# GpSimd's next planned operation waits for each VectorE addition of two SBUF tensors: a linear-attention plus gated-MLP kernel on one core

## The chip, the core and the metric

One core of a Trainium2 chip runs the whole kernel in one launch. The metric is the device time of one execution in microseconds (us); the time given for a kernel is the median of several executions. The core has five engines with their own instruction queues, each worked off in order: PE (TensorE), ACT (ScalarE), DVE (VectorE), POOL (GpSimd) and SP (SyncE, which here only issues DMAs). They meet through semaphores.

## What is computed

The reference, cut to what matters; S = 2048 tokens, D = 512, H = 32 heads of 16, F = 1792, bfloat16.

```python
xn = layernorm(x)
# A: linear attention with softmax features
q, k, v = split_heads(xn @ wqkv)
phi_q = concat(softmax(q @ w_phi), softmax(-(q @ w_phi)))     # per head, 32 features
phi_k = concat(softmax(k @ w_phi), softmax(-(k @ w_phi)))
kv, z = phi_k^T @ v, sum over tokens of phi_k
a = ((phi_q @ kv) / (phi_q . z + 1e-6)) @ wo
# B: bilinear gated MLP
h = (xn @ w_gate) * (xn @ w_up)
b = h @ w_down
return x + a + b
```

## The kernel before

**Stages.** Tokens are cut into 16 tiles of 128. The kernel warms TensorE up, normalises x tile by tile (LN), and transposes it so that the model dimension lies on the partitions. While the tiles arrive it runs, per token tile t, the features of k (step names `k`, then `ke` two exponentials on ACT, `kr` the sums of the features on DVE (L923), `kc` a reciprocal on ACT, `kq` and `kp` two products on POOL (L930, L935)) and the scaled v (`vs`, DVE, L962), and adds each tile to the state on PE (`kv`). The same for q is `q`, `qe`, `qr`, `qc`, `qq`, `qp`, then a DMA transpose `qT` and the numerators `n` on PE. In between PE does the products for g and u of the MLP, and from about 116 us on the last products, h times w_down and attention times wo, for pairs of token tiles p.

**Seven products instead of eight.** The large matrix products are done in blocks of two by two with seven block products. That needs sums and differences of blocks of both factors beforehand, in SBUF. On these turns the change:

- `Xs` (function XSUMS): eight differences of halves of the transposed xn, [128 x 512] each, on DVE, at 39.6 to 46.1 us. PE's block products `b7g.0` and `b6g.0` read them.
- `Xz` (XPAIR): four more of the same size for the last quarter of the tokens, on DVE, at 97.9 to 100.4 us.
- `S3`, `S1`, `S2`, `S4` (SSUMS) with the pair's number p: sums of halves of h. POOL makes them for p below 6, DVE for p = 6 and 7 ([128 x 896] each), at 180.1 to 195.3 us.
- `w` (WSUMS, L1066), `Ts`, `To`, `So`: sums of weights and of the attention's output, on POOL.

All but `w` are recorded by the helper `sums`, so they share line 989, on DVE and on POOL alike. Of a block product on PE, `b7g.0` say, b7 is the number of the product, g or u the matrix and 0 the block of F; its results are taken from PSUM by ACT (`sd`, `s2`, `s7`, `ge`) and by DVE (`a4`, `a5` at L1086, `h` at L1080).

**What sets the order.** The program is recorded as steps with their reads and writes. A planner (`_plan`) goes through them in one global order, which is written out as a list of step numbers (`ORDER`); from it follows the order of every engine's queue. The dependencies are turned into semaphore waits afterwards. A DVE sum made by `sums` is marked `lock`: in the planner's estimate POOL does not start beside it. That alone makes no wait on the chip. A real wait is added only where the step also has `sync`: the planner then remembers the sum and makes a later POOL step depend on it. The number `slip` says how many POOL steps later that is: 1 is the next POOL step in the global order, 2 the one after it. With `slip` above 1 the next POOL step also gets a dependency on the POOL step just before it, so that POOL has to finish one before it starts the other.

```python
            for q in port:
                if q[2] and last_pool is not None and last_pool not in st.deps:
                    st.deps.append(last_pool)
                q[2] = False
                q[1] -= 1
                if q[1] <= 0 and q[0] not in st.deps:
                    st.deps.append(q[0])
            port = [q for q in port if q[1] > 0]
```

In the kernel before, `sync` holds for sums given an explicit priority, which among the twenty sums on DVE are the eight S sums of pairs 6 and 7, with a slip of 2. The twelve `Xs` and `Xz` have none.

Of the kernel before, what the change touches and what calls it, by code (L numbers as in the profile page):

```python
# [478 lines left out]
AB = {7: (2, 3)}  # L479
CO = {}  # L480
CH = ''
SLIP = 2
SYN = (".0", ".1")
NX = 7
ZORD = '1726453'
# [166 lines left out]
def _program(sc, layout, arena, psum, spill, A_x, A_wqkv, A_w_phi, A_wo, B_w_gate, B_w_up, B_w_down, out):  # L652
# [33 lines left out]
    def dve(fn, reads, writes, cost=None, prio=0, name="", win=60.0):  # L686
        n = max(ap.free_size() for ap in list(writes) + list(reads))
        if cost is None:
            cost = 60.0 + 1.045 * n
        return sc.step(DVE, fn, reads=reads, writes=writes, cost=cost, prio=prio, name=name, win=win)  # L690

    def pool(fn, reads, writes, cost, prio=0, name=""):
        return sc.step(POOL, fn, reads=reads, writes=writes, cost=cost, prio=prio, name=name)
# [291 lines left out]
    def parts(v):  # L985
        return [v[:, k, :] for k in range(v.shape[1])]

    def sums(eng, out_, a_, b_, op, name, prio=None):
        fn = lambda e: e.tensor_tensor(out=out_, in0=a_, in1=b_, op=op)  # L989
        n = out_.free_size()  # L990
        if eng == POOL:
            pool(fn, parts(a_) + parts(b_), parts(out_), 100.0 + 2.0 * n, name=name, prio=prio or 0)
        else:
            st = dve(fn, parts(a_) + parts(b_), parts(out_), cost=60.0 + 0.53 * n, name=name, prio=PX if prio is None else prio)
            st.lock = True
            st.sync = prio is not None
            st.slip = SLIP
            st.reserve = RX if prio is None else 0.0

# [45 lines left out]
    def XSUMS(eng):  # L1045
        X1, X2, X3, X4 = (Tx_v[:, w] for w in range(4))
        for n, (o_, a_, b_) in enumerate(((X1, xB(0, 2), xB(0, 1)), (X3, xB(1, 2), xB(0, 2)), (X2, xB(1, 2), X1),
                                          (X4, xB(1, 1), X2))):
            for k in range(2):
                sums(eng, o_[:, k:k + 1], a_[:, k:k + 1], b_[:, k:k + 1], ALU.subtract, f"Xs{n}.{k}")  # L1050
# [114 lines left out]
    def XPAIR(eng, T_v, s0, name):  # L1165
        X1, X2, X3, X4 = (T_v[:, w] for w in range(4))

        def B(k, c):
            return xnT_v[:, 2 * k:2 * k + 2, s0 + c * 256:s0 + c * 256 + 256]
        for n, (o_, a_, b_) in enumerate(((X1, B(0, 1), B(0, 0)), (X3, B(1, 1), B(0, 1)), (X2, B(1, 1), X1),  # L1170
                                          (X4, B(1, 0), X2))):
            sums(eng, o_, a_, b_, ALU.subtract, f"{name}{n}", None if eng == DVE else 0)
# [172 lines left out]
    def TSUMS():  # L1345
        for n, (o_, a_, b_) in enumerate(((T1, B12, B11), (T2, B22, T1), (T4, B21, T2), (T3, B22, B12))):
            for lo, hi in ((0, 2), (2, 4), (4, 6), (6, HF)):
                sums(POOL, o_[:, lo:hi], a_[:, lo:hi], b_[:, lo:hi], ALU.subtract, f"Ts{n}.{lo}")
# [421 lines left out]
```

## Time and profile before

| what | value |
|---|---|
| three runs | 208.77, 208.51, 208.11 us; median 208.51 |
| the profiled execution | 208.06 us in all, its span 206.3 us |
| granted TensorE clock | 1.00 |
| PE busy | 200.9 us (97%) |
| DVE busy | 175.8 us (85%) |
| POOL busy | 163.6 us (79%) |
| ACT busy | 127.5 us (62%) |
| DVE sums at L989 | 20, 12.7 us busy, mean 671 ns |
| POOL sums at L989 | 92, 85.1 us busy, mean 952 ns |

The span is the time from the first to the last instruction of one profiled execution; the execution's own time is 1.76 us longer. The profile's busy time of PE is not PE at its peak, since matmuls overlap in their pipeline and their ends are modelled. Where the text below gives the times of a single step, they are those of its record in the trace, matched to the step by its place in its engine's queue.

### The profile page before, as it was taken

Reading aid. Unit: us, or ns where it says so; the run is one execution under the profiler, and the core shown is the slowest. Engines: PE = TensorE matmul, PEld = TensorE weight load, DVE = VectorE, ACT = ScalarE, POOL = GpSimd, SP = SyncE. Lnnn points to the kernel's source line nnn. Section 1 sums busy time; section 2 is a strip of 40 time slices with the busy share of each in tenths; the row PEclk is TensorE's granted clock in tenths of the full one; section 3 lists DMA queues with packets and bytes.
Section 4 is the critical chain, followed back from the end, with each engine's and each line's share of the span. In section 5 each row is a group of like instructions: output and inputs, shape, how many; then the busy total and the mean of one; then the engine's idle time right before and its main releaser. Section 6 shows DMA issues by size and latency. Waiting matters only on the chain.

```text
span 206.3 us, 4296 instructions
## 1 busy us (share of the span) xinstructions
PE 200.9 (97%) x1569; PEld 133.2 (65%) x1586; DVE 175.8 (85%) x336; ACT 127.5 (62%) x318; POOL 163.6 (79%) x215
## 2 busy tenths in 40 slices
PE   8999999999999999999999999999999999999995
PEld 2775544444455444544345678979988988998884
DVE  4745999999897899799999899699888769999952
ACT  4666899988787889788786663665653365610000
POOL 4065677449999989999989999999999989996100
PEclk9999999999999999999999999999999999999999
DMA  5999944899002200225672332984965749454212
GB/s 142 332 242 373 337 97 97 192 335 253 7 0 102 102 3 2 102 51 95 182 234 53 105 78 49 144 215 122 253 164 136 149 146 161 134 127 85 71 38 89
DMA packets 52277, 28.87 MB, mean 140 GB/s; under 512 B 37664, under 2 KB 50464, under 8 KB 52256
## 3 DMA queue, kind: packets, MB, share of 16 engines
q1 hardware_dynamic: 51584, 28.27, 53.1%
q10 hardware_dynamic: 672, 0.33, 0.5%
q8 instruction: 12, 0.20, 0.4%
q14 instruction: 9, 0.07, 0.1%
HBM read 13.91 MB, written 5.77 MB: 95 GB/s over the span
## 4 chain that ended last, share of the span: by engine, by line
PE 91%; DVE 5%; ACT 1%; issue 1%; DVEq 0%
PE ps L711 88%; DVE arena L989 2%; PE ps L1536 2%; ACT arena L672 1%; DVE arena L923 1%; DVE arena L1395 1%; DVE arena L1210 0%; DVE arena L1080 0%; DVE arena L1329 0%; DVE arena L962 0%; DVEq L455 0%; DVE arena L1458 0%; DVEq L426 0%; DVE arena L1021 0%
## 5 line engine op out<-in xcount | busy, mean ns | idle before, releaser
L711 PE MATMUL ps<-arena 128*128 128x256 f16 (+5 forms) x1559 | 196.7, 287 | 2.1 <-DVE arena L989 0.4
L711 PEld LDWEIGHTS ps<-arena 128*128 128x128 f16 (+1 forms) x1576 | 131.9, 98 | 67.4 <-DVE arena L1080 2.0
L672 ACT ACTIVATE arena<-ps 128x512 bf16<-128x512 f32 (+3 forms) x184 | 91.6, 538 | 45.2 <-PE ps L711 30.5
L989 POOL TENSOR_TENSOR arena<-arena 128x512 f16<-128x512 f16 (+4 forms) x92 | 85.1, 952 | 8.0 <-DVE arena L834 3.8
L923 DVE TENSOR_REDUCE arena<-arena 128x64 f32<-128x1024 bf16 x32 | 38.7, 1210 | 2.2 <-ACT arena L672 2.2
L935 POOL TENSOR_TENSOR arena<-arena 128x512 bf16<-128x512 bf16 x32 | 34.0, 1067 | 0.4
L1066 POOL TENSOR_TENSOR arena<-arena 128x512 f16<-128x512 bf16 (+1 forms) x28 | 32.3, 1161 | 2.3 <-ACT arena L672 1.1
L672 ACT ACTIVATE arena<-arena 128x32 f32<-128x32 f32 (+4 forms) x96 | 28.4, 314 | 5.4 <-DVE arena L923 3.8
L1395 DVE TENSOR_TENSOR arena<-ps,arena 128x256 bf16<-128x256 f32 (+1 forms) x56 | 22.8, 418 | 6.3 <-PE ps L711 5.6
L1080 DVE TENSOR_TENSOR arena<-ps,arena 128x512 f16<-128x512 f32 x28 | 19.2, 686 | 0.7 <-PE ps L711 0.2
L672 ACT ACTIVATE ps<-ps 128x512 f32<-128x512 f32 x21 | 12.2, 585 | 4.2 <-PE ps L711 2.1
L832 DVE BATCH_NORM_STATS2 arena<-arena 128x6 f32<-128x512 bf16 x16 | 10.5, 674 | 4.3 <-DMA arena<-in_A_x_dram 4.2
L1210 DVE TENSOR_TENSOR arena<-ps,arena 128x256 f16<-128x256 f32 x28 | 11.3, 416 | 3.4 <-ACT arena L672 3.2
L930 POOL TENSOR_TENSOR arena<-arena 128x32 f32<-128x32 f32 x32 | 8.5, 268 | 6.6 <-ACT arena L672 6.6
L989 DVE TENSOR_TENSOR arena<-arena 128x512 f16<-128x512 bf16 (+1 forms) x20 | 12.7, 671 | 0.1
L1086 DVE TENSOR_TENSOR arena<-ps,arena 128x512 bf16<-128x512 f32 x14 | 9.6, 687 | 2.9 <-ACT arena L672 1.5
L962 DVE TENSOR_TENSOR arena<-ps,arena 128x512 bf16<-128x512 f32 x16 | 10.9, 682 | 0.2 <-PE ps L711 0.2
L1329 DVE TENSOR_TENSOR arena<-ps,arena 128x512 bf16<-128x512 f32 x16 | 10.9, 680 | 0.1
L1214 DVE TENSOR_TENSOR ps<-ps,arena 128x512 f32<-128x512 f32 x14 | 9.6, 690 | 0.8 <-PE ps L711 0.5
L1086 DVE TENSOR_TENSOR ps<-ps,arena 128x512 f32<-128x512 f32 x14 | 9.7, 692 | 0.6 <-ACT arena L672 0.6
L814 POOL TENSOR_TENSOR arena<-arena 128x128 bf16<-128x128 bf16 x4 | 1.6, 426 | 8.5 <-DMA arena<-in_A_w_phi_dram 8.5
L1021 DVE TENSOR_TENSOR arena<-ps,arena 128x512 f16<-128x512 f32 x10 | 6.7, 684 | 0.4 <-PE ps L711 0.3
(25 smaller groups left out, 36.5 us busy)
## 6 DMA issues: line engine op xcount, KB each, us to landing
spill<-arena SPq DMA_DIRECT2D x7, 512.0 KB, 2.7
arena<-spill SPq DMA_DIRECT2D x7, 512.0 KB, 3.9
arena<-in_A_x_dram SPq DMA_DIRECT2D x6, 512.0 KB, 5.5
arena<-in_B_w_down_dram SPq DMA_DIRECT2D x2, 896.0 KB, 6.6
out_dram<-arena SPq DMA_DIRECT2D x14, 128.0 KB, 1.9
arena<-in_B_w_gate_dram SPq DMA_DIRECT2D x1, 768.0 KB, 7.6
arena<-in_B_w_up_dram SPq DMA_DIRECT2D x1, 768.0 KB, 7.7
arena<-arena SPq DMA_TRANSPOSE x44, 3.1
```

What stands on the lines that cost most here:

```text
L672: return e.activation(out=out_ap, in_=in_ap, func=func, scale=scale, **kw)
L711: ins = e.matmul(o, lhsT=l, rhs=r, start=s, stop=p, skip_group_check=True)
L923: dve(lambda e: e.tensor_reduce(out=sm, in_=Et.rearrange("p (c h f) -> p c h f", c=8, f=16), axis=AX.X, op=ALU.add), [Et], [sm], cost=1130 ...
L935: pool(lambda e: e.tensor_tensor(out=ev[:, :, 1, :], in0=ev[:, :, 1, :], in1=ratio[:, :, None].to_broadcast([128, H, 16]), op=ALU.mult), [ ...
L962: dve(lambda e: e.tensor_tensor(out=o1, in0=src, in1=rp_[:, :, :, None].to_broadcast([128, 8, 4, 16]), op=ALU.mult), [src, rs_v[:, t % 4, ...
L989: fn = lambda e: e.tensor_tensor(out=out_, in0=a_, in1=b_, op=op)
L1066: pool(lambda e, o_=o_, a_=a_, b_=b_, op=op: e.tensor_tensor(out=o_, in0=a_, in1=b_, op=op), [a_, b_], [o_], 100.0 + 2.09 * 512, name=f"w{ ...
L1080: dve(lambda e: e.tensor_tensor(out=h, in0=src, in1=g, op=ALU.mult), [src, g], [h], name=f"h{ft}.{sg}", prio=PD)
L1086: dve(lambda e: e.tensor_tensor(out=o, in0=src, in1=sn, op=ALU.add), [src, sn], [o], name=name, prio=PD)
L1210: dve(lambda e: e.tensor_tensor(out=h, in0=src, in1=g, op=ALU.mult), [src, g], [h], cost=328.0, name=f"zh{f}.{c}", prio=PB)
L1329: dve(lambda e: e.tensor_tensor(out=ov, in0=src, in1=wv4[:, :, :, None].to_broadcast([128, 8, 4, 16]), op=ALU.mult), [src, w], [o], cost=6 ...
L1395: dve(lambda e: e.tensor_tensor(out=out_, in0=in_ps, in1=in_sb, op=ALU.add), [in_ps, in_sb], [out_], cost=328.0, name=f"{name}.{p}")
```

## The change

All twenty DVE sums now carry `sync`, and the slip is 1: the POOL step that comes next after a sum in the global order waits for that sum. The dependency of a POOL step on the POOL step before it, which went with a slip of 2, is no longer added. The global order, the engines' queues and every computation stay as they are.

```diff
-SLIP = 2
+SLIP = 1
...
             st = dve(fn, parts(a_) + parts(b_), parts(out_), cost=60.0 + 0.53 * n, name=name, prio=PX if prio is None else prio)
             st.lock = True
-            st.sync = prio is not None
+            st.sync = True
             st.slip = SLIP
             st.reserve = RX if prio is None else 0.0
```

In the planned order the POOL steps that follow the sums are these:

| DVE sums | next POOL step (waits after) | wait of before |
|---|---|---|
| Xs1.0, Xs0.0, Xs0.1, Xs1.1 | kq3 | none |
| Xs2.1, Xs2.0, Xs3.0 | kq4 | none |
| Xs3.1 | w3.2 | none |
| Xz0 | qq2 | none |
| Xz2, Xz1, Xz3 | qp2 | none |
| S3.6 | So1.5 | So3.5 |
| S1.6, S3.7, S2.6 | S4.5.3 (fourth sum of pair 5, second part) | So1.6 |
| S4.6, S1.7 | So2.6 | So4.6 |
| S2.7 | So4.6 | none left |
| S4.7 | none left | none left |

## The prediction

> **What bounds the kernel.** I read the page first, then the chain of waits, then both engines of the change in the timeline.
>
> ```profile
> span 206.3 us, 4296 instructions
> PE 200.9 (97%) x1569; PEld 133.2 (65%) x1586; DVE 175.8 (85%) x336; ACT 127.5 (62%) x318; POOL 163.6 (79%) x215
> ```
>
> PE is the bound. So the change can gain only where PE stands still, and can lose wherever it makes PE stand still. The chain that ended last shows where another engine holds PE; its columns are start, us, what:
>
> ```profile
> 39.65 2.38 DVE arena L989 x4
> 42.02 0.04 issue
> 42.07 1.72 PE ps L711 x14
> ...
> 98.33 2.03 DVE arena L989 x3
> 100.36 0.61 DVE arena L1080
> 100.97 0.05 issue
> 101.02 1.47 PE ps L711 x6
> ```
>
> Both places are runs of DVE sums at L989: first Xs, which PE's b7g.0 waits for, then Xz, behind which DVE's h5.1 (L1080) is queued, which PE's k14 waits for. To size PE's standstill I take the starts of successive matmuls less 213 ns, which is the spacing of the 512-column ones elsewhere. It is 0.57 us before b7g.0 at 42.07, 0.17 before k5 at 43.80, 0.50 before k14 at 101.02 and 0.26 before k15 at 102.35. Other pieces over 0.15 us after 10 us are nearly all of 0.22, a missing record each.
>
> Why the sums are late shows in the timeline (start, us, engine), DVE then POOL, and in the group of Xs:
>
> ```profile
> 39.65 2.37 DVE L989 TENSOR_TENSOR arena<-arena 128x512 f16<-128x512 bf16 x4
> ```
> ```profile
> 39.60 0.27 POOL L930 TENSOR_TENSOR arena<-arena 128x32 f32<-128x32 f32 x1 [1.48 <-ACT arena L672]
> 39.95 1.12 POOL L935 TENSOR_TENSOR arena<-arena 128x512 bf16<-128x512 bf16 x1
> ```
> ```profile
> L989 DVE TENSOR_TENSOR arena<-arena x8: 409/456/1272, 39.6 to 45.5; 128x512 f16<-128x512 bf16 x8
> ```
>
> The same sum takes 409 to 1272 ns. The long one is Xs0.0, 40.07 to 41.34: it lies beside kp3 (39.95 to 41.07) and ends 0.28 us behind it. Xz1 does the same beside qp2 (98.68 to 99.96, qp2 ends 99.68: again 0.28), and S3.7 beside S4.5.3 (1570 ns, against 611 for S4.6 with nothing beside it). It goes the other way too: S4.5.3 begins while S1.6 runs and takes 1413 ns against 1150, and So1.5 behind S3.6 929 against 667. So whichever of the two began first keeps the other waiting nearly to its end. Three sums lose 0.86, 0.86 and 0.96 us in this way.
>
> **The change part by part.** The wait makes the order of the plan real: kq3 waits for four Xs, kq4 for three, qq2 and qp2 for the Xz, four POOL steps near the end for S sums.
>
> First place, Xs. With kq3 held, the four sums run at their undisturbed pitch (0.335 us, as Xs0.1 to Xs1.1) from 39.65, so Xs1.1 ends at 39.65 + 3 x 0.335 + 0.41 = 41.06 instead of 42.01. b7g.0 is then ready before PE is: 0.57 gone. DVE goes on 0.95 earlier with kr4 and vs3 (to 42.85 instead of 43.74), so k5's 0.17 is gone as well, minus about 0.03 of normal spacing: 0.7 us. What is late next: kq3, from 39.60 to 41.06 + 0.14 = 41.20 (0.14 us lies between the end of S1.7 and So4.6, which waits for it); kp3 then ends at 42.6, not 41.07, and nb14 and nb15, queued behind it, at 43.2, not 42.14. Their readers come later: kv3 at 50.07, nm14 at 46.32, nm15 at 48.73. kq4 was idle for 2.26 us before 44.40, waiting for ACT's kc4; all that is early brings kc4 to about 43.8 and Xs3.0 to 43.96, so kq4 starts near 44.1. Xs3.1 then meets kp4 and is held to 45.75, before b4g.0 needs it (46.8). w3.2 begins 0.25 us behind b7u.0 on PE, hence 0.7 earlier too; S1.0.3 behind it can't start before the transpose xT13 lands at 47.12 (before: 47.76, directly behind w3.2), so POOL enters the next stretch 0.6 earlier. Thus all engines move together:
>
> ```profile
> 47.00:97.00 50.00, 49.68 (x293) 24.20 (x298) 44.74 (x62) 40.66 (x97) 49.03 (x55) 1.00 0.26 66
> ```
>
> (Columns: stretch, length, busy PE, PEld, DVE, ACT, POOL, granted clock, DMA.) PE and POOL are both full here, and PE's smallest reserves against POOL are 0.14 (w3.4 to b7g.4 at 79.9) and 0.25 us (kp5 to kv5 at 61.4). POOL being 0.1 behind PE's move fits in. I keep 0.69 at 97.
>
> Second place, Xz. Undisturbed they end at 99.42 instead of 100.36; h5.1 ends at 100.02, h12.1 at 101.35, so the 0.50 and 0.26 go. From there DVE's own queue (qr3, kr14, h5.2) is 0.73 earlier, and PE's b1u.6 waits for it with 0.05 to spare: gain 0.73. The price is on POOL:
>
> ```profile
> 98.49 1.18 POOL L935 TENSOR_TENSOR arena<-arena 128x512 bf16<-128x512 bf16 x1
> 99.64 0.45 POOL L930 TENSOR_TENSOR arena<-arena 128x32 f32<-128x32 f32 x1
> 100.04 1.33 POOL L1066 TENSOR_TENSOR arena<-arena 128x512 f16<-128x512 bf16 x1
> 101.33 1.05 POOL L935 TENSOR_TENSOR arena<-arena 128x512 bf16<-128x512 bf16 x1
> ```
>
> qp2 starts at 99.56, 1.07 later; qp2, kq13 and w4.6 get back 0.12, 0.18 and 0.17 of their own stretching, so what is queued behind them (kp13, kp12, S2.0.3 ...) is about 0.6 late (1.07 - 0.12 - 0.18 - 0.17). kv12 on PE has 1.37 us against kp12, which the delay and PE's gain just use up. The transpose qT2 on SP, with a spill store and a load behind it, waits for qp2; the nearest reader of the load has 3.5 us. At 106.99 POOL idles 0.73 us before qq3, and 0.15 before kq15 at 110.61; that takes up the delay and leaves POOL 0.28 ahead of its old place, PE wanting 0.73 (the first part moves both alike). kv14 has 0.30 against kp14, of which 0.05 is signalling: 0.73 - 0.28 - 0.25 = 0.2 comes back there as a new stall, and 0.53 is left of this place.
>
> Third place, the end. S3.7 and S2.6 are 0.95 earlier, S4.5.3 ends at 188.5 instead of 187.2; P3.5 needs it at 192.2. So2.6 is held until S1.7, that is from 189.8 to about 191.6; P6o.6 needs it at 194.8. So4.6 behind it is 0.9 late; P3o.6 comes at 200.5. PE waits there only for c22.5 before P3.5, about 0.1: gain 0.1. The dropped waits of POOL on itself (0.12 us of idle time each, three of them) are hidden under POOL's slack at the end. Each added wait instruction costs POOL at least nothing and at most the 0.08 idle seen before a held step; that is in the 0.14.
>
> Sum: 0.69 + 0.53 + 0.1 = 1.32. Against its own execution 208.06 becomes 206.7; that execution is 0.45 below the median, and from the median 208.51 I get 207.2.
>
> The Trainium skill, SBUF — State Buffer, "Who interferes with whom", calls the shared pair of ports an exclusive lock, held for a whole instruction by the one that issued first, and lets DVE operations with two SBUF inputs take part. The rows above agree. By this rule the wait saves no time on the ports, it only moves it from DVE to POOL; with POOL as the bound it would give the last rival's time.
>
> **The rivals.** One: the first gain is lost again in the stretch from 47 to 97. The waits put w3.2's idle 0.78 us to a transpose (L1066 waiting for arena<-arena), and xT12 does land at 46.61. If that, and not b7u.0, starts POOL, POOL is not earlier, and b7g.4 cuts PE's gain to 0.1. Then the sum is 0.1 + 0.5 + 0.1 = 0.7: 207.8. Against it: w3.2 reads nothing of xT12; S1.0.3 behind it does.
>
> Two: nothing measurable. PE regains the stalls and gives them up at other waits with 0.05 us to spare, of which there are some thirty; 208.5.
>
> Three, slower: POOL's delay reaches PE through kp. If the Xz do not shorten (their length then has another cause than their neighbour), qp2 starts at 100.36 + 0.14, 2.0 late; kp12 ends 1.66 late, and kv12 with its 1.37 stalls 0.35; past the 0.73 and 0.15 of idle time 0.78 is left, kv14 with 0.25 stalls 0.53 in all. No gain at the first place either: 208.51 + 0.5 = 209.0. It decides once POOL is over 1.37 us late against PE at kv12 or 0.30 at kv14. For it: POOL is 98% busy from 47 to 97. Against it: twice 0.28 us between the neighbour's end and the sum's.
>
> **How the numbers follow.** Forecast 0.50, rival one 0.18, rival two 0.15, rival three 0.17. A difference of about 0.3% (0.6 us) is what can be told from none. Rival one lies just beyond that bound; forecast and rival one make faster 0.68, rival two same 0.15, rival three slower 0.17. Low end: all of PE's stalls go, 0.70 + 0.76 + 0.15 = 1.6, so 206.9, less 0.3 for the spread of the runs (208.11 to 208.77): 206.6. High end: rivals one and two are in, 208.7; left out is most of rival three. The forecast's own range is 206.8 to 207.5.
>
> **What would show it.** Right: no DVE sum of 512 columns over 0.6 us except Xs3.1; Xs1.1 ends near 41.1; b7g.0, k5, k14 and k15 without standstill; qp2 about 1 us behind qc2's end; PE's piece at 47 to 97 moved by 0.7. Wrong: PE waiting for L935 (kp) at kv12 or kv14; kp5 or w3.4 as PE's releaser; sums as long as before.

## The result and the profile after

The changed kernel takes 206.64 us (median of six runs), the kernel before 208.65 in the same comparison: ratio 0.990, interval 0.988 to 0.992, so 2.0 us faster (1.6 to 2.5). The prediction was 207.2 us, with a range of 206.8 to 207.5 for the forecast alone and 206.6 to 208.7 with its rivals, and a gain of 1.3 us. Two more comparisons, told below as experiments, gave 0.994 (0.992 to 0.996) and 0.992 (0.989 to 0.995). A ratio here is worked out from all runs of its comparison; it is not the quotient of the two medians and differs from it by up to 0.0013. Over all four sets of runs the median of 24 runs with the change is 206.62 and of 92 without it 208.06: 1.45 us.

The page, first lines:

```profile
span 205.1 us, 4301 instructions
PE 200.1 (98%) x1569; PEld 133.2 (65%) x1586; DVE 173.6 (85%) x336; ACT 127.3 (62%) x318; POOL 162.6 (79%) x215
```

DVE is 2.2 us less busy with the same 336 instructions. The chain that ended last (start, us, what) no longer leaves PE at either place:

```profile
30.17 10.74 PE ps L711 x49
40.91 0.05 issue
40.96 7.19 PE ps L711 x53
...
92.14 9.27 PE ps L711 x49
101.41 0.05 issue
101.46 8.22 PE ps L711 x51
```

The two breaks of 0.05 us that it still lists there are matmuls whose record is missing (in v3 and in k15), not waits. The group of the eight Xs, and the timeline of DVE and of POOL at the first place:

```profile
L989 DVE TENSOR_TENSOR arena<-arena x8: 415/418/1251, 39.8 to 44.7; 128x512 f16<-128x512 bf16 x8
```
```profile
39.83 1.42 DVE L989 TENSOR_TENSOR arena<-arena 128x512 f16<-128x512 bf16 x4
...
42.93 1.21 DVE L989 TENSOR_TENSOR arena<-arena 128x512 f16<-128x512 bf16 x3
...
44.66 1.25 DVE L989 TENSOR_TENSOR arena<-arena 128x512 f16<-128x512 bf16 x1
```
```profile
41.33 0.27 POOL L930 TENSOR_TENSOR arena<-arena 128x32 f32<-128x32 f32 x1 [3.04 <-ACT arena L672]
41.68 1.06 POOL L935 TENSOR_TENSOR arena<-arena 128x512 bf16<-128x512 bf16 x1
...
44.23 0.27 POOL L930 TENSOR_TENSOR arena<-arena 128x32 f32<-128x32 f32 x1 [0.50 <-DVE arena L989]
```

The first four sums take 1.42 us instead of 2.37, and kq3 (L930) starts behind them, at 41.33 instead of 39.60. The profile puts its wait down to ACT, but ACT's kc3 had ended at 39.70; Xs1.1 ended at 41.25, 0.08 us before kq3 starts, and that is the wait that was added. The one long sum left, 1251 ns, is Xs3.1 beside kp4.

The four Xz at the second place, first in the kernel before, then with the change:

```profile
97.88 2.48 DVE L989 TENSOR_TENSOR arena<-arena 128x512 f16<-128x512 bf16 x4
```
```profile
97.31 1.60 DVE L989 TENSOR_TENSOR arena<-arena 128x512 f16<-128x512 bf16 x4
```

POOL there, with the change:

```profile
98.99 1.05 POOL L935 TENSOR_TENSOR arena<-arena 128x512 bf16<-128x512 bf16 x1 [0.69 <-DVE arena L989]
100.01 0.26 POOL L930 TENSOR_TENSOR arena<-arena 128x32 f32<-128x32 f32 x1
100.23 1.15 POOL L1066 TENSOR_TENSOR arena<-arena 128x512 f16<-128x512 bf16 x1
101.34 1.06 POOL L935 TENSOR_TENSOR arena<-arena 128x512 bf16<-128x512 bf16 x1
```

qp2 is held until the Xz are done; behind it kq13 and w4.6 are back at 0.26 and 1.15 us (0.45 and 1.33 before), so that kp13 starts at 101.34, as before (101.33). PE, though, comes to kv12, which needs the next product kp12, 1.16 us earlier than in the trace before (103.62 instead of 104.77).

To compare two traces I take the start of one PE step in both. The steps just ahead of the first place differ already: v3, which reads no sum and starts before the first of them ends, lies between 39.73 and 40.51 us in twelve profiled executions of all the kernels here, in no relation to the change. Behind v3 there is hardly any spread: the time of the whole execution less the start of v3 is 168.14 and 168.15 us in the two profiled executions of the kernel before, and 166.70, 166.70 and 166.68 in the three with the change. Counted from v3, the change moves PE in three stretches only:

| PE's place against the kernel before, us | first place (v3 to b5g.0) | second (q3 to b5g.6) | end (P4.5 to P4.7) | v3 to P4.7 |
|---|---|---|---|---|
| before, a second profile | 0.00 | 0.00 | -0.03 | -0.03 |
| with the change, three profiles | -0.75, -0.76, -0.75 | -0.59, all three | -0.12, -0.12, -0.11 | -1.46, all three |
| Xs alone | -0.75 | 0.00 | -0.03 | -0.78 |
| Xz alone | 0.00 | -0.59 | -0.03 | -0.62 |
| S alone | 0.00 | 0.00 | -0.11 | -0.12 |
| the sums wait instead | +0.18 | +1.12 | +0.06 | +1.45 |
| slip of 2 for all | -0.75 | -0.07 | -0.03 | -0.85 |
| qp2 later still | -0.75 | +0.28 | -0.11 | -0.47 |

The last column can differ from the sum of the others by what is lost between the second place and the end: 0.09 where the sums wait, 0.11 with qp2 later still.

### The profile page after: what moved, and what is told of

Same layout as the page of the kernel before. It is cut to its first block, busy times and chain, and to the rows that moved or that the text cites. A ratio compares the mean times of both kernels' runs of the same rounds, so it can differ in the third digit from the quotient of the medians.

```text
span 205.1 us, 4301 instructions
## 1 busy us (share of the span) xinstructions
PE 200.1 (98%) x1569; PEld 133.2 (65%) x1586; DVE 173.6 (85%) x336; ACT 127.3 (62%) x318; POOL 162.6 (79%) x215
## 4 chain that ended last, share of the span: by engine, by line
PE 92%; DMA 2%; DVE 2%; ACT 1%; issue 1%; POOL 0%; DVEq 0%; POOLq 0%
PE ps L711 92%; DMA arena<-in_B_w_up_dram 2%; ACT arena L672 1%; DVE arena L923 1%; DVE arena L1395 1%; DVE arena L1210 0%; DVE arena L1329 0%; POOL arena L778 0%; POOL arena L805 0%; DVEq L455 0%; DVE arena L1458 0%; POOL arena L777 0%; POOLq L778 0%; POOL arena L806 0%; POOLq L1755 0%
## 5 line engine op out<-in xcount | busy, mean ns | idle before, releaser
L989 POOL TENSOR_TENSOR arena<-arena 128x512 f16<-128x512 f16 (+4 forms) x92 | 84.5, 943 | 9.8 <-DVE arena L989 4.3
L935 POOL TENSOR_TENSOR arena<-arena 128x512 bf16<-128x512 bf16 x32 | 33.7, 1059 | 1.0 <-DVE arena L989 0.7
L832 DVE BATCH_NORM_STATS2 arena<-arena 128x6 f32<-128x512 bf16 x16 | 10.5, 674 | 5.2 <-DMA arena<-in_A_x_dram 5.2
L930 POOL TENSOR_TENSOR arena<-arena 128x32 f32<-128x32 f32 x32 | 8.5, 269 | 5.3 <-ACT arena L672 4.7
L989 DVE TENSOR_TENSOR arena<-arena 128x512 f16<-128x512 bf16 (+1 forms) x20 | 10.5, 562 | 0.1
```

The lines of the kernel that those rows point to most:

```text
L935: pool(lambda e: e.tensor_tensor(out=ev[:, :, 1, :], in0=ev[:, :, 1, :], in1=ratio[:, :, None].to_broadcast([128, H, 16]), op=ALU.mult), [ ...
```

## The experiments

Theory: a sum and a POOL step that overlap block each other, and the wait lets the sum go first at places where PE is behind the sum and nothing close is behind the POOL step. Against it: that POOL's delay comes back at PE; that avoiding the overlap counts, whoever waits; that the gain lies somewhere no trace shows.

**The kernel before once more.** No edit but `SLIP = 1 + 1`.

> The kernel before, unchanged: a second profile and more runs of it, since the two profiled executions differ by 1.3 us and the medians by 2.0. If the collisions of sums and GpSimd steps are the same in every execution, this profile shows Xs0.0 and Xz1 at 1.27 us again, the same standstills of PE (0.57 before b7g.0, 0.50 before k14), a span near 206.3 us and a time near 208.1. If they vary from run to run and the profiled execution was a lucky one, more sums are long here and the span is near 206.9. If the start varies (arrival of the inputs), the sums are as in the first profile and the span differs before 39 us.

208.16 us against 207.99, ratio 1.000 (0.9985 to 1.0015). The group of Xs:

```profile
L989 DVE TENSOR_TENSOR arena<-arena x8: 410/456/1275, 40.0 to 45.9; 128x512 f16<-128x512 bf16 x8
```

The same eight durations within 4 ns, and Xz1 at 1281. So the collisions of Xs and Xz belong to the order, not to chance. Of the S sums S3.7 is long again (1578 ns), but S3.6 takes 616 ns and not 844, so that one does vary. What varies in the whole time is the start (v3 at 40.32 instead of 39.92), which is the whole of the 0.4 us between this span (206.7) and the first (206.3).

**Each place alone.**

```diff
-            st.sync = prio is not None
-            st.slip = SLIP
+            st.sync = prio is not None or name.startswith('Xs')
+            st.slip = 1 if name.startswith('Xs') else SLIP
```

> Only the eight Xs are waited for (kq3, kq4, w3.2). Collision theory: the 0.57 and 0.17 us of PE's standstill at 42 to 44 us go, nothing else: 0.75 us faster than before, ratio 0.996. Rival one of the prediction (GpSimd not earlier, the gain given back at b7g.4): 0.1 us, ratio 0.9995. If the measured 2.0 us come mostly from this place: 1.4 us or more, ratio 0.993.

207.17 us, ratio 0.996 (0.994 to 0.998). The eight Xs, then the four Xz, in two views of the same line of code:

```profile
L989 DVE TENSOR_TENSOR arena<-arena x8: 416/418/1247, 39.5 to 44.3; 128x512 f16<-128x512 bf16 x8
```
```profile
L989 DVE TENSOR_TENSOR arena<-arena x4: 419/453/1276, 97.0 to 99.0; 128x512 f16<-128x512 bf16 x4
```

The Xs are short, Xz1 is long as before, and PE gains 0.75 us that it keeps to the end. With `'Xz'` in place of `'Xs'`:

> Only the four Xz are waited for (qq2, qp2). Collision theory: the 0.50 us before k14 goes, ratio 0.9975. If GpSimd's delay takes part of it back at kv12 or kv14: 0.3 us, ratio 0.9985. If the measured 2.0 us come mostly from this place: over 1 us, ratio 0.995.

207.40 us, ratio 0.9975 (0.9957 to 0.9994).

```profile
L989 DVE TENSOR_TENSOR arena<-arena x4: 410/421/476, 97.7 to 98.9; 128x512 f16<-128x512 bf16 x4
```

The Xs have their 1274 ns again, the Xz are at most 476. PE gains 0.59: the whole of its standstill, nothing comes back.

With `st.sync` as before and `st.slip = 1`, so that only the S sums' waits change:

> Only the eight S sums of pairs 6 and 7 are waited for one step earlier; Xs and Xz have no wait, as before. Collision theory: S3.7 at 0.61 instead of 1.57 us, GpSimd's S4.5.3 1.3 us later, both under cover; PE gains the 0.1 us before P3.5: ratio 0.9995, cannot be told from no change. If the end of the kernel depends on those sums: 0.5 to 1.0 us, ratio 0.996.

207.91 us, ratio 0.998 (0.996 to 1.000), not told from no change; in the trace 0.11 us.

```profile
L989 DVE TENSOR_TENSOR arena<-arena x8: 611/617/781, 179.9 to 194.4; 128x896 f16<-128x896 f16 x8
```

S3.7 went from 1570 to 612 ns, the largest saving of a single sum here, and is worth 0.1 us: PE's P7.7, which reads it, began 1.33 us behind its end even in the kernel before. The 0.1 us is PE's P3.5, which waited for c22.5, a step behind the S sums in DVE's queue. The three places, 0.75, 0.59 and 0.11, add up to 1.45 us, the change's own 1.46.

**The changed kernel again**, `SLIP = 2 - 1`, beside the two that follow:

> The changed kernel once more, on one chip with the three below. In the traces so far the three places add up: 0.77 (Xs alone), 0.57 (Xz alone), 0.13 us (S alone), 1.47 together, and 1.46 in the changed kernel's own trace once its later start is taken off. If that is the whole effect, the ratio is 0.993 and the 2.0 us of the first comparison were partly the spread of six runs against six. If there is something that the profiled executions do not show, it is 0.990 again.

206.73 against 208.03 us, ratio 0.994 (0.992 to 0.996): 1.3 us by the medians. The same 1.46 us in the trace.

**The other side waits.** In the kernel before, after the planning, with `by` the steps by name:

```diff
+    [by[late].deps.append(by[first]) for late, first in (("Xs0.0", "kp3"), ("Xz1", "qp2"), ("S3.7", "S4.5.3"))]
```

> The kernel before, with the order of the pairs turned round by a wait of the other side: Xs0.0 waits for kp3, Xz1 for qp2, S3.7 for S4.5.3, so that neither meets its neighbour, and VectorE pays. If the gain comes from avoiding the collision as such (both engines at full speed), it is faster: ratio 0.995. If it comes from who goes first, PE's standstills before b7g.0 and k14 stay and grow by the 0.15 to 0.2 us of the signal and of the 0.41 us sum behind it: 0.3 to 0.4 us slower than before, ratio 1.002.

209.74 us, ratio 1.0085 (1.006 to 1.011): slower, and by more than expected. DVE in the timeline:

```profile
41.69 1.10 DVE L989 TENSOR_TENSOR arena<-arena 128x512 f16<-128x512 bf16 x3 [0.95 <-POOL arena L935]
...
100.48 1.77 DVE L989 TENSOR_TENSOR arena<-arena 128x512 f16<-128x512 bf16 x2 [0.95 <-POOL arena L935]
```

At the first place it goes as reckoned: three sums at full speed in 1.10 us, but from 41.69 on; PE loses 0.18. At the second, Xz1 let qp2 by and Xz3 behind it then met the next POOL step, w4.6: Xz3 took 1370 ns, and PE lost 1.12. So avoiding a collision was not enough: the first place lost time although its sums ran at full speed. What gained here was to let the side go first that PE was waiting behind; and a wait can make the next collision, as at the second place.

**The wait one step later.** The changed kernel with `SLIP = 2`.

> All twenty sums carry a wait, but with a slip of 2: the second GpSimd step after a sum waits. By the planned order kp3 is then held for the Xs (kq3 is not), but qp2 only for Xz0, and S4.5.3 not at all. Collision theory: Xs0.0 short, Xz1 and S3.7 long again; the gain is that of the first place, 0.7 us, ratio 0.9965. If any wait of GpSimd suffices: 0.993 as with the change.

207.30 us, ratio 0.998 (0.995 to 1.000): not told from no change by the times, in the trace 0.85 us.

```profile
L989 DVE TENSOR_TENSOR arena<-arena x4: 412/422/1280, 97.1 to 99.1; 128x512 f16<-128x512 bf16 x4
```

As the planned order says, kp3 is held and Xs0.0 is short (414 ns), qp2 is held for Xz0 alone and Xz1 is long. The 0.07 us at the second place is Xz3, which takes 412 ns instead of 482, since kq13 now waits for it. The full 0.75 us of the first place is there although kq3, the small product, still runs beside Xs1.0 (498 ns): that overlap costs PE nothing.

**How much delay POOL can take.** The changed kernel, and `by["qp2"].deps.append(by["a4u.5"])`.

> The changed kernel with GpSimd's delay at the second place made larger: qp2 waits also for a4u.5 on VectorE, which ended at 100.12 us, so that qp2 starts 1.2 us later than in the changed kernel (98.99). The prediction's third rival: GpSimd's delay reaches PE through kp12 and kv12. In the changed kernel's trace kp12 ends 0.20 us before kv12's first weights are loaded; 0.05 of that is signalling, so 1.2 - 0.15 = 1.05 us of new standstill before kv12, and the kernel is 1.0 us slower than the changed one: ratio 0.998 against before. If GpSimd's delay is hidden as before: no change against the changed kernel.

207.55 us, ratio 0.997 (0.996 to 0.9985); 0.8 us slower than the changed kernel's 206.73 in the same comparison, 0.99 in the trace. The chain that ended last now runs through POOL:

```profile
99.89 0.07 issue
99.95 1.06 POOL arena L935
101.01 0.23 POOL arena L930
101.24 1.12 POOL arena L1066
102.36 2.04 POOL arena L935 x2
104.45 5.86 PE ps L711 x40
```

kp12 ends at 104.39 and PE's kv12, which waits for it, starts behind it: 0.87 us of PE's gain goes there and 0.12 more at kv14. So the prediction's third rival names a real mechanism, and the change lies 0.2 us short of it.

**A third comparison, and the last long sum.** The changed kernel again, and the changed kernel with `by["kp4"].deps.append(by["Xs3.1"])`.

> The changed kernel a third time, beside fresh runs of the kernel before, because the first two comparisons gave 0.990 and 0.994. The traces give 1.46 us from 39 us to the end in every pair looked at, ratio 0.993; if the excess of the first comparison is in the runs of the kernel before (208.65 there, 208.0 twice since), the changed kernel reads 206.6 to 206.8 and the kernel before 208.0 again: 0.9935. If the change has a part that no trace shows, 0.990.

206.42 against 208.09 us, ratio 0.992 (0.989 to 0.995); 1.46 us in the trace once more.

> The changed kernel, with kp4 also waiting for Xs3.1, the one sum of 512 columns that is still long (1251 ns, ending with kp4). If a long sum costs time only where PE waits behind it: Xs3.1 becomes 0.42 us and ends 0.8 us earlier, its reader b4g.0 (1.0 us later) does not move, kp4 ends 0.6 us later with w3.2 behind it 0.1 us later: no change, or up to 0.1 us slower. If every avoided collision counts, 0.8 us faster than the changed kernel, ratio 0.990.

206.44 us, ratio 0.992 (0.989 to 0.994).

```profile
L989 DVE TENSOR_TENSOR arena<-arena x8: 415/418/425, 39.7 to 44.5; 128x512 f16<-128x512 bf16 x8
```

Not one of the eight is long any more, and neither the time (206.42 without this wait) nor PE's place (1.46) moves. So a long sum costs time only where PE is waiting behind it. No version here beats the changed kernel.

## Why the prediction was right or wrong

The direction, the mechanism and the places were right; the time was not: 207.2 us was forecast, 206.64 measured. Two steps made the difference, and the larger is not in the mechanism.

The step that failed is the level from which the gain was taken. The prediction's terms come from one profiled execution of 208.06 us; it called that execution 0.45 us below the median and took its 1.32 us off 208.51, the median of the three runs that it had. The later runs show that the profiled execution was an ordinary one: 86 of them, on two chips, have a median of 208.05 us, and only 13 reach 208.51. From 208.06 the same sum gives 206.74.

The smaller step is the sum itself, 1.32 us where every trace shows 1.46: it lacked 0.06 us at each of the first two places and 0.02 at the end. From 208.06 the 1.46 gives 206.60.

The 2.0 us of the first comparison (1.6 to 2.5) exclude both 1.32 and 1.46; the two others gave 1.3 and 1.7 by their medians. The excess is in the first comparison's six runs of the kernel before (median 208.65; 207.99, 208.03 and 208.09 later, while the changed kernel stayed within 206.42 to 206.73), and three of those six were the prediction's level. No trace shows an effect of the change beyond the 1.46. What made those six runs slow stays open: v3's start varies by 0.8 us from execution to execution, which would be enough, but those runs have no profile, nor is it known on which chip they ran.

- *First term, 0.69.* It measured 0.75, the whole 0.57 and 0.17. The prediction took 0.03 off for a normal spacing and kept 0.69 of the rest without a reason for the last hundredths; neither was lost. (The normal spacing in the trace is 216 ns and not 213, which changes no standstill by more than 0.003 us.) POOL moved with PE through the full stretch: 0.70 earlier at w3.2, and PE's smallest reserve against it at b7g.4 is 0.14 as before. That also answers rival one: PE keeps its 0.75 up to q3.
- *Second term, 0.53.* It measured 0.59, but by other parts than the prediction gave. Of the two standstills, 0.50 and 0.26, the second was misread: at the same k15 the trace after also has a piece of 0.22, a missing record, so that only 0.04 was standstill; the rest of the 0.59 are hundredths at the steps behind. And the 0.2 us that I let come back at kv14 did not: with PE wanting 0.59 and not 0.73, POOL's earlier start behind qq3 and kq15 (its idle 0.73 and 0.15 are gone) was just enough, kp14 ending 0.10 us before kv14's weights load. That two errors cancel to 0.06 is luck.
- *Third term, 0.1.* It measured 0.11 to 0.12.
- *POOL's price.* qp2 came 1.08 us late, counted from PE's q3 (forecast 1.07). kv12 was left 0.20 of its 1.37 us; forecast was nearly nothing, the difference being what PE wanted less. So2.6 and S4.5.3 came 1.7 us late against PE and were covered, as said. The signal from a sum's end to the held step took 0.08 us, not 0.14.
- *Rival two* (gains lost at waits with 0.05 us to spare): it falls, because all engines moved together; between the three places PE's shift changes by no more than 0.04.
- *Rival three:* its condition, sums that stay long, did not hold. Its path is real, as the later qp2 showed.
- *The exclusive lock* (the Trainium skill, SBUF — State Buffer, "Who interferes with whom"): by this rule, as the prediction worked it out, the waits only move time from DVE to POOL. The traces agree: the busy time of the twenty sums fell by 2.2 us (12.7 to 10.5), POOL's waits for them at L989 and L935 rose from 1.5 to 5.0, and PE's gain came from where the waiting was put. One figure the prediction passed over: Xs0.0 ended 0.28 us behind kp3, while an undisturbed sum takes 0.41, so some 0.13 us of it was not held back (an estimate from these two figures).
- *What would show it:* Xs1.1 ended at 41.25 with a start 0.18 later (forecast 41.06), Xs3.1 at 45.91 (45.75), kq4 began at 44.23 (44.1); no other sum of 512 columns is over 0.48 us.

## What to carry to other kernels

Where VectorE operations on two SBUF tensors and GpSimd operations meet, look at the longest duration of a group beside its shortest (here 1272 ns beside 409), and ask which of the two sides the bound engine is waiting behind; a wait that lets that side go first delays the other side's queue (here kq3 by 1.6 us and qp2 by 1.1) and is worth it only if the readers behind that queue have the reserve. Count that reserve to the reader before adding such a wait (here 1.37 us, of which 0.2 was left). Shortening an operation that nobody is waiting behind gained nothing here, even where it took 1.25 us down to 0.42 (Xs3.1).

## What was not expected of the hardware

The size of the start's spread: at a granted clock of 0.999 to 1.00 the kernels here, whose work on PE is the same up to there, reach the same PE step (v3) between 39.73 and 40.51 us, while from there to P4.7 three executions of the changed kernel agree within 0.01 us (159.36). The transfers of the inputs vary too: the 768 KB of w_up take 10.0 us to land in the profile with the change (the line below), 7.7 in that of before. But the two don't go in step (8.1 us with v3 at 40.32 in the second profile of the kernel before, 8.9 us with v3 at 39.73 in the second with the change), so that what sets the start isn't shown.

```profile
arena<-in_B_w_up_dram SPq DMA_DIRECT2D x1, 768.0 KB, 10.0
```

And a small POOL product that starts just behind one sum still meets the next one: qq2, held for Xz0 alone, took 494 ns instead of 269 beside Xz2 and Xz1, without a price, since qp2 behind it was held anyway.
